# Windowed attention beside a gated MLP: probabilities of units 3 to 15 transposed by VectorE and two transfers through DRAM in place of TensorE

## The chip, the core and the metric

One core of a Trainium2 chip. TensorE (PE in the profile) multiplies matrices into PSUM; VectorE (DVE), ScalarE (ACT) and GpSimd (POOL) work element by element; SyncE (SP) issues all transfers. Each engine runs its own instructions in their written order and waits on semaphores for the others. The metric is the device time of one execution in microseconds, the median of three runs.

## What is computed

```python
scores = scale * np.matmul(q, k.transpose(0, 1, 3, 2))      # 8 batches, 8 heads, 576 positions, 64 wide
mask_plain = (rel >= 0) & (rel < window)                    # heads 0-3: the last 32 positions
mask_dil = (rel >= 0) & (rel < window * dilation) & (rel % dilation == 0)   # heads 4-7: every fourth of 128
scores = np.where(masks[None, :, :, :], scores, -1000000000.0)
attn = np.exp(scores - max); attn = attn / (sum + 1e-09)
out = np.matmul(attn, v)
x = out.transpose(0, 2, 1, 3).reshape(B * S, H * D)         # 4608 tokens of 512
rms = np.sqrt(np.mean(x * x, axis=-1, keepdims=True) + 1e-06)
xn = x / rms * rms_g
g = xn @ w_gate; val = xn @ w_val                           # 512 -> 1536
return silu(g) * val @ w_out                                # 1536 -> 512
```

All of it is float32.

## The kernel before

The 4608 tokens are cut into 16 units of 288 (half a batch). While the MLP of one unit runs, the attention of the next is done in between. Float32 products are made of three float32r products: each operand is split into a high part (ScalarE's cast) and a low part (the rest, `k_lo`, `q_lo` L361-L365, `vhl` L324, `hlo` L749 on GpSimd, `xlo` partly on VectorE), and `three` (L674) multiplies high by high, high by low and low by high.

**The MLP's steps.** A unit has 12 blocks of 128 hidden columns, and each block three steps (L858 on): `gate(u, j)`, `val(u, j)`, and `proj` of the block before. Each step is 12 matmuls of 288 columns. Gate and value of a block take two PSUM banks in turn (`bank`, L692): gate of block j+1 writes the bank that value of block j wrote, so its first matmul waits until the product (`prod`, L735, L737: silu(g) times value, VectorE) of block j has read that. Ahead of the product lie ScalarE's tanh (L719) and VectorE's silu (L724); behind it ScalarE's `hhi` (L748) and GpSimd's `hlo` (L749), which the projection needs two steps later.

**The bursts.** A unit's attention is 14 bursts, each one block of queries of two heads: three blocks of 96 queries for each of two pairs of plain heads, four classes of 72 for each of two pairs of dilated heads. A burst named 5_3_1 is unit 5, pair 3, block 1. Its stages: two score matmuls (L524, float32r, the key's high and low part side by side); one step later VectorE adds the mask to the low product (L381) and takes the maximum with the high one (L386); then ScalarE's exp (L401), VectorE's sum and reciprocal (L410, L411), GpSimd's scaling (L417, `scores_norm`). Six steps behind the scores (`BEHIND`), TensorE transposes the probabilities of both heads (L497) into free columns of a gate bank or a bank of its own; ScalarE evicts the high part (L477) and VectorE the low part (L479, `untranspose`). Ten steps behind the scores, the output matmuls (L512) multiply by v's two parts, and VectorE gathers the result (L439, L441, `take`). Bursts follow every second step, from 11 steps ahead of a unit's first gate to 15 after it.

**What sets the order.** The program is written by hand: `later(dt, rank, fn)` puts a piece of work into the list of a later step, `flush` emits a step's list by rank ahead of the step's matmuls, and each engine keeps that order. `plan` (L808) fixes each burst's steps. Units 0 to 2 (`NEX` = 3) do their attention in plain float32 with other code, which the change leaves on TensorE.

Of the kernel before, what the change touches and what calls it, by code (L numbers as in the profile page):

```python
# [14 lines left out]
ALU = mybir.AluOpType  # L15
# [42 lines left out]
EARLY, LAST = -11, 15  # L58
BEHIND = 6, 10
DONE = 25  # L60
# [17 lines left out]
def attn_moe(ctx: ExitStack, tc: tile.TileContext, qk_in, v_in, w_gate, w_val, w_out, rms_g, outT):  # L78
# [235 lines left out]
    def split_v(b, dt):  # L314
        k = everything.index(b) % 2

        def hi():
            if k not in vparts:
                vparts[k] = late[0].tile([P, 2, 2, D], F32R, name=f"vhl_{k}", bufs=1)
            A.copy(out=vparts[k][:, :, 0], in_=vs[b])  # L320

        def lo():
            vp = vparts[k]
            G.tensor_tensor(out=vp[:, :, 1], in0=vs.pop(b), in1=vp[:, :, 0], op=ALU.subtract)  # L324
            load_v(further(b, 3))

        later(dt, 3.3, hi)
        later(dt, 5.1, lo)
# [6 lines left out]
    def split(u, h, when, ek, eq):  # L335
# [11 lines left out]
        def k_hi():  # L347
            ks = tile(2 * KW, "ks").rearrange("p (t k) -> p t k", t=2)
            A.copy(out=ks[:, 0, :nkt], in_=kr)
            got.append(ks)  # L350

        def k_lo():
            ks = got[0]
            ek.tensor_tensor(out=ks[:, 1, :nkt], in0=kr, in1=ks[:, 0, :nkt], op=ALU.subtract)  # L354

# [5 lines left out]
        def q_lo():  # L361
            ks, qs = got
            eq.tensor_tensor(out=qs[D:], in0=qr[D:], in1=qs[D:], op=ALU.subtract)  # L363
            heads[u, h] = (qs, ks)
            if after(u, h, 2):  # L365
                load(*after(u, h, 2))

# [6 lines left out]
    def scores_max(u, c, i, s_ps):  # L374
        blocks, nq, _ = geometry(u, c)
        _, _, mc, n = blocks[i]
        sv = s_ps[:QB].rearrange("q (a t k) -> q a t k", a=2, t=2)
        other = u < NNAT and everything.index((u, c, i)) % 4 == 3
        t = sb.tile([QB, 2, P], F32, tag="qs" if other else "t", name=f"t_{u}_{c}_{i}", bufs=3)
        if u >= NEX:  # L380
            V.tensor_tensor(out=t[:nq, :, :n], in0=sv[:nq, :, 1, :n],  # L381
                            in1=mask[:nq, None, mc:mc + n].to_broadcast([nq, 2, n]), op=ALU.add)
        sm = sums[everything.index((u, c, i)) % len(sums)]
        for a in range(2):
            plus = t[:nq, a, :n] if u >= NEX else mask[:nq, mc:mc + n]
            V.tensor_tensor_reduce(out=t[:nq, a, :n], in0=sv[:nq, a, 0, :n], in1=plus,  # L386
                                   op0=ALU.add, op1=ALU.min,
                                   scale=-(0.5 if u == NNAT else 1.0) / math.sqrt(D),
                                   scalar=3e38, accum_out=sm[:nq, a, 0:1])
        st[u, c, i] = t, sm  # L390

    def by_rows(u, c, i):
# [3 lines left out]
    def scores_exp(u, c, i):  # L396
        blocks, nq, _ = geometry(u, c)
        n = blocks[i][3]
        t, sm = st[u, c, i]
        for a in range(2):  # L400
            A.activation(out=t[:nq, a, :n], in_=t[:nq, a, :n], func=AF.Exp, scale=-1.0,  # L401
                         bias=sm[:nq, a, 0:1], accum_out=None if by_rows(u, c, i) else sm[:nq, a, 1:2])

    def scores_norm(u, c, i):
# [65 lines left out]

    def untranspose(b, t_ps, wait):
        blocks, nq, _ = geometry(*b[:2])
        n = blocks[b[2]][3]
        t_in = t_ps[:n].rearrange("k (a q) -> k a q", a=2)[:, :, :nq]
        exact = b[0] < NEX
        st[b] = pt = sb.tile([P, 2, 2, QB], F32 if exact else F32R, tag="pt", name=f"pt_{b[0]}_{b[1]}_{b[2]}", bufs=2)
        A.copy(out=pt[:n, 0, :, :nq], in_=t_in)  # L477
        def low_part():
            V.tensor_tensor(out=pt[:n, 1, :, :nq], in0=t_in, in1=pt[:n, 0, :, :nq], op=ALU.subtract)  # L479

        if not exact:
            later(1, 0.4 if wait > 1 else -1.5, low_part) if wait else low_part()

    def products(q, t, o, t_ps, s_tag="s", o_tag="o", wait=0):
# [30 lines left out]
        def scored(a):  # L515
# [7 lines left out]
            qs, ks = heads[q[0], 2 * q[1] + a]  # L523
            PE.matmul(sv[:nq, a, :, :n], qs[:, qc:qc + nq], ks[:, :, kc:kc + n], start=True, stop=True)  # L524
# [8 lines left out]
        if t:  # L533
            later(1, 0.2, lambda: untranspose(t, t_ps, wait))
        if o:
# [322 lines left out]
    for u in range(NU):  # L858
        for j in range(NJ):
            for part in range(0 if u + j else 2, 3):  # L860
# [16 lines left out]
                else:  # L877
# [79 lines left out]
```

## Time and profile before

| | |
|---|---|
| median of three runs | 1105.96 us (1104.24 to 1106.1) |
| profiled execution | 1103.95 us; its span 1102.2 us |
| granted TensorE clock | 1.00 of full speed |
| GpSimd's busy time, hlo (L749) and both splits (L354, L363) | 145.2, 96.8 and 84.3 us of 670.1 |
| VectorE's busy time, silu and products (L724, L737), gathering (L439, L441) | 80.8 and 79.8, 117.1 and 101.1 us of 782.7 |
| DMA | 82.18 MB, mean 75 GB/s |

How to read it: a row in order of time has its start and length in us, engine, line, operation, output and inputs, and in brackets how long the engine stood idle before it and what ended that. A row of a group ends in its busy time in us, the mean length of one in ns, and idle time before. A row of stretches gives each engine's busy time (and instructions) in order PE, PE's weight loads, DVE, ACT, POOL, then the granted clock, the DMA share and GB/s. Matmuls overlap, so one's length says little; the distance from start to start says what it costs.

### The profile page before, as it was taken

Reading aid. Unit: us, or ns where it says so; the run is one execution under the profiler, and the core shown is the slowest. Engines: PE = TensorE matmul, PEld = TensorE weight load, DVE = VectorE, ACT = ScalarE, POOL = GpSimd, SP = SyncE. Lnnn points to the kernel's source line nnn. Section 1 sums busy time; section 2 is a strip of 40 time slices with the busy share of each in tenths; the row PEclk is TensorE's granted clock in tenths of the full one; section 3 lists DMA queues with packets and bytes.
Section 4 is the critical chain, followed back from the end, with each engine's and each line's share of the span. In section 5 each row is a group of like instructions: output and inputs, shape, how many; then the busy total and the mean of one; then the engine's idle time right before and its main releaser. Section 6 shows DMA issues by size and latency. Waiting matters only on the chain.

```text
span 1102.2 us, 25627 instructions
## 1 busy us (share of the span) xinstructions
PE 1095.2 (99%) x8416; PEld 1071.6 (97%) x8416; DVE 782.7 (71%) x3094; ACT 614.8 (56%) x2202; POOL 670.1 (61%) x1152
## 2 busy tenths in 40 slices
PE   8999999999999999999999999999999999999998
PEld 7787999999999999999999999999999999999998
DVE  7988667868687676867768677686867768687412
ACT  6895676556465564646556464664646556464211
POOL 6333589657585675757657575775758657584211
PEclk9999999999999999999999999999999999999999
DMA  9774213212131131312212131131212212120000
GB/s 255 205 263 163 79 51 87 74 35 82 43 94 52 41 97 30 95 42 73 66 36 85 43 94 43 50 96 37 79 43 83 64 32 83 53 74 13 18 6 22
DMA packets 61543, 82.18 MB, mean 75 GB/s; under 512 B 7298, under 2 KB 41090, under 8 KB 61410
## 3 DMA queue, kind: packets, MB, share of 16 engines
q1 hardware_dynamic: 61410, 80.54, 24.3%
q8 instruction: 67, 1.10, 0.4%
q14 instruction: 66, 0.54, 0.2%
HBM read 71.08 MB, written 9.44 MB: 73 GB/s over the span
## 4 chain that ended last, share of the span: by engine, by line
PE 95%; POOL 2%; DVE 1%; ACT 1%; issue 1%; POOLq 0%; ACTq 0%; DVEq 0%
PE acc L682 17%; PE g L682 17%; PE v L682 17%; PE acc L679 9%; PE g L679 9%; PE v L679 9%; PE o L512 3%; PE s L524 3%; PE acc L676 2%; PE v L676 2%; PE g L676 2%; PE t L497 2%; PE s L521 1%; PE g L497 1%; PE busy L802 1%; PE o L509 1%
## 5 line engine op out<-in xcount | busy, mean ns | idle before, releaser
L749 POOL TENSOR_TENSOR hlo<-th,hhi 128x288 fp32r<-128x288 f32 x179 | 145.2, 811 | 161.3 <-ACT hhi L748 147.8
L401 ACT ACTIVATE t<-t,sum 96x128 f32<-96x128 f32 (+3 forms) x448 | 165.9, 374 | 107.8 <-DVE sum L386 105.1
L682 PE MATMUL acc<-hhi,lo 128*128 128x288 f32 x720 | 212.7, 295 | 0.0
L417 POOL TENSOR_SCALAR t<-t,sum 96x128 f32<-96x128 f32 (+3 forms) x416 | 147.6, 366 | 88.4 <-DVE sum L411 74.6
L719 ACT ACTIVATE th<-g 128x288 f32<-128x288 f32 x180 | 73.8, 410 | 195.2 <-PE g L682 100.5
L682 PE MATMUL g<-xhi,lo 128*128 128x288 f32 x612 | 180.3, 295 | 0.0
L682 PE MATMUL v<-xhi,lo 128*128 128x288 f32 x612 | 180.2, 294 | 0.0
L439 DVE TENSOR_REDUCE xraw<-o 64x72 f32<-64x144 f32 (+1 forms) x364 | 117.1, 322 | 84.0 <-PE o L512 79.5
L724 DVE SCALAR_TENSOR_TENSOR th<-th,g 128x288 f32<-128x288 f32 x180 | 80.8, 449 | 102.0 <-ACT th L719 78.4
L682 PEld LDWEIGHTS acc<-hhi,lo 128*128 128x128 f32 x720 | 135.4, 188 | 0.0
L324 POOL TENSOR_TENSOR vhl<-vt,vhl 128x128 fp32r<-128x128 f32 x182 | 84.4, 464 | 70.4 <-ACT vhl L320 66.8
L748 ACT CAST hhi<-th 128x288 fp32r<-128x288 f32 x180 | 77.7, 432 | 75.5 <-DVE th L737 74.6
L682 PEld LDWEIGHTS g<-xhi,lo 128*128 128x128 f32 x612 | 115.2, 188 | 0.0
L682 PEld LDWEIGHTS v<-xhi,lo 128*128 128x128 f32 x612 | 115.1, 188 | 0.0
L737 DVE TENSOR_TENSOR th<-th,v 128x288 f32<-128x288 f32 x180 | 79.8, 444 | 43.6 <-PE v L682 43.5
L441 DVE TENSOR_TENSOR xraw<-o,xraw 64x72 f32<-64x72 f32 (+1 forms) x364 | 101.1, 278 | 12.5
L679 PE MATMUL acc<-hhi,hi_o 128*128 128x288 f32 x360 | 109.0, 303 | 0.0
L679 PE MATMUL g<-xhi,hi_g 128*128 128x288 f32 x357 | 107.0, 300 | 0.0
L682 PE MATMUL acc<-hlo,hi_o 128*128 128x288 f32 x360 | 106.4, 296 | 0.0
L363 POOL TENSOR_TENSOR qs<-qk,qs 64x288 fp32r<-64x288 f32 x104 | 84.3, 811 | 24.1 <-ACT qs L358 16.9
L354 POOL TENSOR_TENSOR ks<-qk,ks 128x288 fp32r<-128x288 f32 (+2 forms) x104 | 96.8, 936 | 3.1
L682 PE MATMUL g<-xlo,hi_g 128*128 128x288 f32 x322 | 95.1, 295 | 0.0
(193 smaller groups left out, 3458.6 us busy)
## 6 DMA issues: line engine op xcount, KB each, us to landing
qk<-in_qk_dram SPq DMA_DIRECT2D x60, 288.0 KB, 2.9
vt<-in_v_dram SPq DMA_DIRECT2D x196, 64.0 KB, 1.9
qk<-in_qk_dram SPq DMA_DIRECT2D x30, 352.0 KB, 2.9
out_dram<-ot SPq DMA_DIRECT2D x64, 144.0 KB, 1.9
qk<-in_qk_dram SPq DMA_DIRECT2D x30, 304.0 KB, 2.9
raw<-in_w_gate_dram SPq DMA_DIRECT2D x12, 512.0 KB, 4.6
raw<-in_w_val_dram SPq DMA_DIRECT2D x12, 512.0 KB, 3.3
raw<-in_w_out_dram SPq DMA_DIRECT2D x12, 512.0 KB, 4.2
```

The lines of the kernel that those rows point to most:

```text
L324: G.tensor_tensor(out=vp[:, :, 1], in0=vs.pop(b), in1=vp[:, :, 0], op=ALU.subtract)
L354: ek.tensor_tensor(out=ks[:, 1, :nkt], in0=kr, in1=ks[:, 0, :nkt], op=ALU.subtract)
L363: eq.tensor_tensor(out=qs[D:], in0=qr[D:], in1=qs[D:], op=ALU.subtract)
L401: A.activation(out=t[:nq, a, :n], in_=t[:nq, a, :n], func=AF.Exp, scale=-1.0, bias=sm[:nq, a, 0:1], accum_out=None if by_rows(u, c, i) els ...
L417: (V if u == 0 and (c, i) > (NC - 1, 1) else G).tensor_scalar(out=t[:nq, a, :n], in0=t[:nq, a, :n], scalar1=sm[:nq, a, 3:4], scalar2=1.0, ...
L439: V.tensor_reduce(out=ours, in_=o[:D, cols:cols + 2 * nq].rearrange("d (t q) -> d q t", t=2), axis=mybir.AxisListType.X, op=ALU.add)
L441: V.tensor_tensor(out=ours, in0=o[D:, cols:cols + nq], in1=ours, op=ALU.add)
L679: PE.matmul(out, wh[:, cc, :], xh, start=start, stop=False)
L682: PE.matmul(out, w[:, cc, :], v, start=False, stop=stop and k == 1)
L724: V.scalar_tensor_tensor(out=t, in0=t, scalar=1.0, in1=g, op0=ALU.add, op1=ALU.mult)
L737: V.tensor_tensor(out=t, in0=t, in1=v_ps[:, :U], op=ALU.mult)
L749: (V if (u, j) == (NU - 1, NJ - 1) else G).tensor_tensor(out=lo, in0=t, in1=hi, op=ALU.subtract)
```

## The change

From unit 3 on, no burst is transposed by TensorE. Once the probabilities are scaled, VectorE transposes the tile of 96 queries by 2 x 128 keys in squares of 32 x 32, in place. A first transfer writes it to DRAM (2 x 96 rows of 512 bytes), and a second, which waits for the first, reads it back with the key on the partition, in pieces of 32 queries (768 pieces of 128 bytes). ScalarE casts the high part and VectorE makes the low part, as before, but from SBUF. The stages stand at steps 5, 5, 6, 9 and 9 behind the scores (`TURN`); the output stays at 10.

So that the second transfer finds keys in order, keys are kept in four classes: the splitting of k reads every fourth column and writes the classes one after another (L346 on), the scores' moving operand has eight runs in place of two, and the mask is rearranged once. Tiles whose burst has fewer than 96 queries or 128 keys are first filled with zeros by GpSimd (`begin`), when the scores are issued. One more tile of probabilities is kept, one less for v (two, not three); the loads of q, k and v are put one step later, behind the transfers.

```diff
-BEHIND = 6, 10
+OUTPUT = 10
+TURN = (5, 4), (5, 9.5), (6, 9.5), (9, 0.2), (9, 0.9)
...
-            vt = sb.tile([P, 2, D], F32, tag="vt", name=f"vt_{u}_{c}_{i}", bufs=3)
+            vt = sb.tile([P, 2, D], F32, tag="vt", name=f"vt_{u}_{c}_{i}", bufs=2)
...
-            A.copy(out=ks[:, 0, :nkt], in_=kr)
+            A.copy(out=ks[:, 0, :nkt].rearrange("p (c k) -> p c k", c=4), in_=kr.rearrange("p (k c) -> p c k", c=4))
...
-            ek.tensor_tensor(out=ks[:, 1, :nkt], in0=kr, in1=ks[:, 0, :nkt], op=ALU.subtract)
+            hi, lo = (ks[:, t, :nkt].rearrange("p (c k) -> p c k", c=4) for t in range(2))
+            ek.tensor_tensor(out=lo, in0=kr.rearrange("p (k c) -> p c k", c=4), in1=hi, op=ALU.subtract)
...
-                load(*after(u, h, 2))
+                later(1, 9.9, lambda: load(*after(u, h, 2)))
...
+            t = blank.pop((u, c, i))
+            tk, mk = keys(t, n), mask.rearrange("q (c k) -> q c k", c=4)[:, :, mc // 4:(mc + n) // 4]
...
+            V.tensor_tensor(out=tk[:nq], in0=low[:nq], in1=mk[:nq].to_broadcast(list(tk[:nq].shape)), op=ALU.add)
...
+    def begin(b):
+        _, nq, _ = geometry(*b[:2])
+        n = geometry(*b[:2])[0][b[2]][3]
+        pool, bufs = (late[0], 1) if late and everything.index(b) % 4 == 3 else (sb, 3)
+        blank[b] = t = pool.tile([QB, 2, P], F32, tag="t", name=f"t_{b[0]}_{b[1]}_{b[2]}", bufs=bufs)
+        if nq < QB or n < P:
+            G.memset(t, 0.0)
...
+    def turn(b):
...
+        def squares():
+            t = st[b][0]
+            V.transpose(out=t, in_=t)
+        def put():
+            t, _ = st.pop(b)
+            d = dr.tile([2, QB, P], F32, tag="turn", name=f"turn_{b[0]}_{b[1]}_{b[2]}")
+            nc.sync.dma_start(out=d.rearrange("a q k -> q a k"), in_=t)
+            got.append(d)
+        def get():
+            st[b] = pt = sb.tile([P, 2, 2, QB], F32R, tag="pt", name=f"pt_{b[0]}_{b[1]}_{b[2]}", bufs=2)
+            squares = got.pop().rearrange("a (r i) (c j) -> (i c) (a r) j", i=W, j=W)
+            nc.sync.dma_start(out=pt[:, 1].bitcast(F32).rearrange("k a (r j) -> k (a r) j", j=W), in_=squares)
+        def high():
+            pt = st[b]
+            A.copy(out=pt[:n, 0, :, :nq], in_=pt[:n, 1, :, :nq].bitcast(F32))
+        def low():
+            pt = st[b]
+            V.tensor_tensor(out=pt[:n, 1, :, :nq], in0=pt[:n, 1, :, :nq].bitcast(F32), in1=pt[:n, 0, :, :nq], op=ALU.subtract)
+        for (dt, rank), fn in zip(TURN, (squares, put, get, high, low)):
+            later(dt, rank, fn)
...
+            kk = ks[:, :, :nkt].rearrange("p t (c k) -> p t c k", c=4)[..., kc // 4:(kc + n) // 4]
...
-        t_at, o_at = ([t + n for t in q_at] for n in BEHIND)
+        t_at, o_at = [None] * nb, [t + OUTPUT for t in q_at]
```

**Where instructions move.** The first place is GpSimd, around the low parts of the next unit's k while the scores of 5_3_1 are made (`hlo_4_3` is the hidden block 3 of unit 4; `ks_6_0` and `ks_6_1` are k of unit 6, `qs` its q, `t` the probabilities). Before:

```order
L749 TENSOR_TENSOR hlo_4_3_5038<-th_4_3_4995,hhi_4_3_5037 128x288
L354 TENSOR_TENSOR ks_6_0_5008<-qk_6_0_4812,ks_6_0_5008 128x288
L354 TENSOR_TENSOR ks_6_1_5010<-qk_6_1_4849,ks_6_1_5010 128x288
L363 TENSOR_TENSOR qs_6_0_5041<-qk_6_0_4812,qs_6_0_5041 64x288
L324 TENSOR_TENSOR vhl_0_2294<-vt_5_2_2_4890,vhl_0_2294 128x2x64
L417 TENSOR_SCALAR t_5_3_0_5004<-t_5_3_0_5004,sum0_86 72x104 x2
L363 TENSOR_TENSOR qs_6_1_5081<-qk_6_1_4849,qs_6_1_5081 64x288
```

And with the change, at the same place:

```order
L812 TENSOR_TENSOR hlo_4_3_5112<-th_4_3_5070,hhi_4_3_5111 128x288
L357 TENSOR_TENSOR ks_6_0_5082<-qk_6_0_4916,ks_6_0_5082 128x288
L357 TENSOR_TENSOR ks_6_1_5084<-qk_6_1_4959,ks_6_1_5084 128x288
L418 MEMSET t_5_3_1_5141 96x256
L366 TENSOR_TENSOR qs_6_0_5115<-qk_6_0_4916,qs_6_0_5115 64x288
L326 TENSOR_TENSOR vhl_0_2300<-vt_5_2_2_5047,vhl_0_2300 128x2x64
L447 TENSOR_SCALAR t_5_3_0_5068<-t_5_3_0_5068,sum0_88 72x4x26 x2
L366 TENSOR_TENSOR qs_6_1_5154<-qk_6_1_4959,qs_6_1_5154 64x288
L418 MEMSET t_5_3_2_5209 96x256
```

A memset of each burst's tile now stands in the queue, behind hlo and whatever part of a split falls into the step.

The second place is VectorE, between the maximum of 5_3_1 and the product of block 4 of unit 4. Before:

```order
L386 ISA t_5_3_1_5074,sum1_87<-s_5_3_1_5058,t_5_3_1_5074 72x104
L386 ISA sum1_87 72x1
L410 TENSOR_REDUCE sum0_86<-sum0_86 72x2
L411 RECIPROCAL sum0_86<-sum0_86 72x2
L724 SCALAR_TENSOR_TENSOR th_4_4_5104<-th_4_4_5104,g_4_4_5087 128x288
L737 TENSOR_TENSOR th_4_4_5104<-th_4_4_5104,v_4_4_5112 128x288
```

With the change:

```order
L400 ISA t_5_3_1_5141,sum1_89<-s_5_3_1_5135,t_5_3_1_5141 72x4x26
L400 ISA sum1_89 72x1
L533 TENSOR_TENSOR pt_5_2_1_5045<-pt_5_2_1_5045 104x2x72
L514 STREAM_TRANSPOSE t_5_2_3_5006<-t_5_2_3_5006 96x256
L439 TENSOR_REDUCE sum0_88<-sum0_88 72x2
L440 RECIPROCAL sum0_88<-sum0_88 72x2
L787 SCALAR_TENSOR_TENSOR th_4_4_5178<-th_4_4_5178,g_4_4_5161 128x288
L800 TENSOR_TENSOR th_4_4_5178<-th_4_4_5178,v_4_4_5190 128x288
```

The low part stands here and not between the gathering instructions, and a transpose in squares is new between the maximum and the product.

The third place is SyncE's queue at the same burst, whose rows were loads alone. Before:

```order
L293 DMA qk_6_0_4812<-in_qk_dram 128x576
L301 DMA vt_5_2_1_4819<-in_v_dram 128x128
L293 DMA qk_6_1_4849<-in_qk_dram 128x576
L301 DMA vt_5_2_2_4890<-in_v_dram 128x128
L301 DMA vt_5_2_3_4953<-in_v_dram 128x128
```

With the change:

```order
L295 DMA qk_6_0_4916<-in_qk_dram 128x576
L303 DMA vt_5_2_0_4918<-in_v_dram 128x128
L519 DMA turn_5_2_0_4957<-t_5_2_0_4783 96x2x128
L295 DMA qk_6_1_4959<-in_qk_dram 128x576
L525 DMA pt_5_2_0_4983<-turn_5_2_0_4957 128x6x32
L303 DMA vt_5_2_1_4985<-in_v_dram 128x128
L519 DMA turn_5_2_1_5025<-t_5_2_1_4864 96x2x128
L525 DMA pt_5_2_1_5045<-turn_5_2_1_5025 128x6x32
```

Each burst has two more transfers there, and the second waits for the first to land and for the output matmuls of the burst two before, with the loads behind it in the queue.

More of the change, by code (lines that the diff above doesn't have):

```diff
@@ L87, in attn_moe @@
     ps = ctx.enter_context(tc.tile_pool(name="ps", bufs=1, space=PSUM))
+    dr = ctx.enter_context(tc.tile_pool(name="dr", bufs=2, space=bass.MemoryType.DRAM))
     ident = cst.tile([QB, QB], F32, name="ident")
@@ L324, in lo @@
             G.tensor_tensor(out=vp[:, :, 1], in0=vs.pop(b), in1=vp[:, :, 0], op=ALU.subtract)
-            load_v(further(b, 3))
+            later(1, 9.9, lambda: load_v(further(b, 2)))
         later(dt, 3.3, hi)
@@ L378, in scores_max @@
         other = u < NNAT and everything.index((u, c, i)) % 4 == 3
[L379 to L382, printed above, removed]
+        if u < NEX:
+            t = sb.tile([QB, 2, P], F32, tag="qs" if other else "t", name=f"t_{u}_{c}_{i}", bufs=3)
+        else:
+            t = blank.pop((u, c, i))
+            tk, mk = keys(t, n), mask.rearrange("q (c k) -> q c k", c=4)[:, :, mc // 4:(mc + n) // 4]
+            low = sv[:, :, 1, :n]
+            if n == P:
+                mk = mk.rearrange("q c i -> q (c i)")[:, None]
+            else:
+                mk, low = mk[:, None], low.rearrange("q a (c i) -> q a c i", c=4)
+            V.tensor_tensor(out=tk[:nq], in0=low[:nq], in1=mk[:nq].to_broadcast(list(tk[:nq].shape)), op=ALU.add)
         sm = sums[everything.index((u, c, i)) % len(sums)]
         for a in range(2):
-            plus = t[:nq, a, :n] if u >= NEX else mask[:nq, mc:mc + n]
-            V.tensor_tensor_reduce(out=t[:nq, a, :n], in0=sv[:nq, a, 0, :n], in1=plus,
+            out, scores, plus = t[:nq, a, :n], sv[:nq, a, 0, :n], mask[:nq, mc:mc + n]
+            if u >= NEX:
+                out = plus = tk[:nq, a]
+                if n < P:
+                    scores = scores.rearrange("q (c i) -> q c i", c=4)
+            V.tensor_tensor_reduce(out=out, in0=scores, in1=plus,
                                    op0=ALU.add, op1=ALU.min,
@@ L390, in scores_max, with keys @@
         st[u, c, i] = t, sm
+    def keys(t, n):
+        return t[:, :, :n] if n == P else t.rearrange("q a (c i) -> q a c i", i=W)[..., :n // 4]
+    blank = {}
+    def begin(b):
[5 more added lines that the diff above has]
+            G.memset(t, 0.0)
     def by_rows(u, c, i):
@@ L469, in attn_moe, with untranspose @@
     everything = [b for u in range(NU) for b in bursts(u)]
-    def untranspose(b, t_ps, wait):
+    def untranspose(b, t_ps):
         blocks, nq, _ = geometry(*b[:2])
         n = blocks[b[2]][3]
[L474 to L482, printed above, removed]
+        st[b] = pt = sb.tile([P, 2, 2, QB], F32, tag="pt", name=f"pt_{b[0]}_{b[1]}_{b[2]}", bufs=2)
+        A.copy(out=pt[:n, 0, :, :nq], in_=t_ps[:n].rearrange("k (a q) -> k a q", a=2)[:, :, :nq])
+    def turn(b):
+        blocks, nq, _ = geometry(*b[:2])
+        n = blocks[b[2]][3]
+        got = []
+        def squares():
[15 more added lines that the diff above has]
+            pt = st[b]
+            V.tensor_tensor(out=pt[:n, 1, :, :nq], in0=pt[:n, 1, :, :nq].bitcast(F32), in1=pt[:n, 0, :, :nq],
+                            op=ALU.subtract)
+        for (dt, rank), fn in zip(TURN, (squares, put, get, high, low)):
+            later(dt, rank, fn)
     def products(q, t, o, t_ps, s_tag="s", o_tag="o", wait=0):
@@ L533, in products @@
         if t:
-            later(1, 0.2, lambda: untranspose(t, t_ps, wait))
+            later(1, 0.2, lambda: untranspose(t, t_ps))
         if o:
@@ L541, in products @@
             if o[0] < NEX:
-                later(1, 9, lambda: load_v(further(o, 3)))
+                later(1, 9, lambda: load_v(further(o, 2)))
             far = further(o, 2)
@@ L551, in products @@
             u, c, i = q
+            if u >= NEX:
+                begin(q)
+                turn(q)
+                if q == (NEX, 0, 0):
+                    t = sb.tile([QB, 2, P], F32, tag="t", name="by_four", bufs=3)[:, 0]
+                    A.copy(out=t.rearrange("q (c k) -> q c k", c=4), in_=mask.rearrange("q (k c) -> q c k", c=4))
+                    A.copy(out=mask, in_=t)
             nxt = after(u, 2 * c, 2)
@@ L810, in plan @@
             for kind, t in zip("qto", ts):
-                events.setdefault(base + t, {})[kind] = b
+                if t is not None:
+                    events.setdefault(base + t, {})[kind] = b
         last = base + (o_at[-1] if u < NNAT else DONE)
@@ L881, in attn_moe @@
                     free = None
-                if part == 2 or part == 1 and events.get(now[0], {}).get("t", (0,))[0] >= NEX:
-                    if "t" in events.get(now[0], {}):
-                        free = ps.tile([P, 512], F32, tag=bank("g", j), name=f"t_{u}_{j}")[:, :2 * QB]
+                if part == 2 and "t" in events.get(now[0], {}):
+                    free = ps.tile([P, 512], F32, tag=bank("g", j), name=f"t_{u}_{j}")[:, :2 * QB]
                 attend(free, s_tag="acc2" if t < 4 else "s", wait=(1, 2, 0)[part])
```

12 lines of the change are left out of this document (7 added, 5 removed).

## The prediction

> **What bounds the kernel now.** I read the page first, then TensorE in order of time, then VectorE and GpSimd in the stretch where attention and the MLP run side by side. The page's first lines and its chain of waits:
>
> ```profile
> span 1102.2 us, 25627 instructions
> PE 1095.2 (99%) x8416; PEld 1071.6 (97%) x8416; DVE 782.7 (71%) x3094; ACT 614.8 (56%) x2202; POOL 670.1 (61%) x1152
> ...
> PE 95%; POOL 2%; DVE 1%; ACT 1%; issue 1%; POOLq 0%; ACTq 0%; DVEq 0%
> ```
>
> TensorE is busy 99% of the span and carries 95% of the chain, so an instruction taken from it shortens the kernel by its own slot, if nothing else becomes late. Whether something does is not read from 71%. From the first output matmuls of a unit to its last scores VectorE has far more to do. The next view is busy time in five stretches of such a passage (columns: TensorE, weight loads, VectorE, ScalarE, GpSimd). Each stretch runs from the end of one product of L737 to the end of the next. The second answer's sum is the same passage one unit earlier, where the keys are the shorter kind:
>
> ```profile
> 320.59:327.54 6.95, 6.95 (x57) 6.95 (x56) 6.43 (x28) 5.60 (x21) 6.06 (x11) 1.00 0.61 184
> 327.54:331.86 4.32, 4.32 (x38) 4.32 (x37) 3.45 (x16) 2.37 (x10) 3.19 (x7) 1.00 0.35 98
> 331.86:338.72 6.86, 6.86 (x57) 6.86 (x55) 5.60 (x26) 3.81 (x16) 2.62 (x6) 1.00 0.09 29
> 338.72:342.98 4.26, 4.26 (x38) 4.26 (x37) 3.36 (x16) 2.87 (x11) 3.98 (x7) 1.00 0.04 12
> 342.98:349.79 6.81, 6.81 (x56) 6.81 (x55) 5.56 (x27) 3.46 (x15) 4.88 (x11) 1.00 0.43 119
> sum 29.20, PE 29.20 PEld 29.20 DVE 24.41 ACT 18.10 POOL 20.73; mean PE 5.84 PEld 5.84 DVE 4.88 ACT 3.62 POOL 4.15
> ```
> ```profile
> sum 28.85, PE 28.85 PEld 28.85 DVE 23.31 ACT 17.36 POOL 19.62; mean PE 5.77 PEld 5.77 DVE 4.66 ACT 3.47 POOL 3.92
> ```
>
> VectorE is 84% busy here, and its instructions start 0.03 to 0.04 us after one another. What it truly waits is only this (one row for each wait; the first stretch has the 0.2, the short ones the two of 0.3 each, the long ones the 0.9):
>
> ```profile
> DVE xraw L439 <- PE o L512: 0.2, 1, 0.2
> DVE th L737 <- PE v L682: 0.3, 1, 0.3
> DVE xraw L439 <- PE o L512: 0.3, 1, 0.3
> DVE xraw L439 <- PE o L512: 0.9, 1, 0.9
> ```
>
> So VectorE's work, gaps between instructions included, is 6.75, 3.7, 5.95, 3.65 and 5.9 us. TensorE needs its product in time: a gate group writes the bank that the product before it reads. The first matmuls of the gate groups:
>
> ```profile
> 322.11 0.30 PE L679 MATMUL g<-xhi,hi_g 128*128 128x288 f32 x1
> ...
> 328.01 0.31 PE L679 MATMUL g<-xhi,hi_o 128*128 128x288 f32 x1
> ...
> 333.34 0.29 PE L679 MATMUL g<-xhi,hi_g 128*128 128x288 f32 x1
> ...
> 339.14 0.31 PE L679 MATMUL g<-xhi,hi_g 128*128 128x288 f32 x1
> ...
> 344.45 0.30 PE L679 MATMUL g<-xhi,hi_v 128*128 128x288 f32 x1
> ...
> 350.01 0.38 PE L679 MATMUL g<-xhi,hi_o 128*128 128x288 f32 x1
> ```
>
> The products end 1.52, 0.47, 1.48, 0.42, 1.47 and 0.22 us ahead of them. Every second margin is under half a microsecond. That is what the change must not use up.
>
> **What it takes away.** One burst (two heads of a block) is two output matmuls, two transposes, two score matmuls. Starts of transposes and scores in a burst of 96 queries and in one of 72, and a row that counts the bursts of the units concerned:
>
> ```profile
> 327.65 0.33 PE L497 MATMUL t<-ident,t 96*128 96x96 f32 x2
> 327.76 0.41 PE L524 MATMUL s<-ks,qs 128*72 128x208 f32 x2
> ...
> 412.01 0.29 PE L497 MATMUL g<-ident,t 72*72 72x72 f32 x2
> 412.10 0.33 PE L524 MATMUL s<-ks,qs 128*72 128x144 f32 x2
> ```
> ```profile
> L324 POOL TENSOR_TENSOR vhl<-vt,vhl 128x128 fp32r<-128x128 f32 x182 | 84.4, 464 | 70.4 <-ACT vhl L320 66.8
> ```
>
> The pair takes 0.11 and 0.09 us of TensorE's time, since matmuls overlap: 0.10. 182 bursts x 0.10 = 18.2 us. The evictions stay: ScalarE's and VectorE's parts of the probabilities now read SBUF, for the same columns.
>
> **What it adds to VectorE.** One transpose in squares for each burst, 96 x 256 elements. No row shows one. The nearest is an addition of the same size; with it, from VectorE in order of time, the reductions and additions that gather an output and the mask addition of burst 3_1:
>
> ```profile
> L381 DVE TENSOR_TENSOR t<-s,mask 96x256 f32<-96x256 f32 x66 | 27.5, 417 | 1.2
> ```
> ```profile
> 327.85 0.35 DVE L439 TENSOR_REDUCE xraw<-o 64x96 f32<-64x192 f32 x1 [0.31 <-PE o L512]
> 328.23 0.26 DVE L441 TENSOR_TENSOR xraw<-o,xraw 64x96 f32<-64x96 f32 x1
> ...
> 339.02 0.30 DVE L439 TENSOR_REDUCE xraw<-o 64x72 f32<-64x144 f32 x1 [0.30 <-PE o L512]
> 339.36 0.29 DVE L441 TENSOR_TENSOR xraw<-o,xraw 64x72 f32<-64x72 f32 x1
> ...
> 340.73 0.37 DVE L381 TENSOR_TENSOR t<-s,mask 72x208 f32<-72x208 f32 x1
> ```
>
> I take 0.42 and the gap, 0.45 us. At the low end 0.30, as the 144-element reduction (one input from SBUF and no arithmetic could be quicker); at the high end 0.85, if a square is written only after it is read. In VectorE's order it stands behind the masked maximum and ahead of the next product, so it lies on the way to the gate group.
>
> **What it adds to GpSimd.** 116 memsets of 96 x 256: in all 13 units for the eight bursts of the dilated heads, and in six for the first blocks of the plain ones. VectorE's mask addition into the same tile waits for it. Memset rows, and GpSimd in order of time before bursts 2_2 and 3_1 of the unit quoted:
>
> ```profile
> L263 POOL MEMSET qk<- 64x576 f32 x5 | 2.6, 572 | 0.1
> ...
> L101 POOL MEMSET mask<- 96x128 f32 x1 | 0.2, 201 | 0.0
> ```
> ```profile
> 328.10 0.81 POOL L749 TENSOR_TENSOR hlo<-th,hhi 128x288 fp32r<-128x288 f32 x1
> 328.99 0.81 POOL L363 TENSOR_TENSOR qs<-qk,qs 64x288 fp32r<-64x288 f32 x1
> ...
> 339.27 0.81 POOL L749 TENSOR_TENSOR hlo<-th,hhi 128x288 fp32r<-128x288 f32 x1
> 340.04 1.58 POOL L354 TENSOR_TENSOR ks<-qk,ks 128x288 fp32r<-128x288 f32 x2
> ```
>
> Between 128 and 576 columns the price grows by 0.83 ns a column, so 0.31 us each. The memset of 2_2 is queued behind hlo and qs: it ends at 328.99 + 0.81 + 0.31 = 330.1. VectorE, once late, does two reductions and two additions after the product that ends at 327.54, 2 x (0.35 + 0.26) and gaps, 1.36 us, and asks for it at 328.9: a wait of 1.2. The memset of 3_1 stands behind hlo and both low parts of k: 340.04 + 1.58 + 0.31 = 341.9. VectorE asks at 338.72 + 2 x (0.30 + 0.29) and gaps = 340.0, a wait of 1.9. Even in this trace the addition started at 340.73, ahead of that end. Behind the waiting addition stand the maximum, the low part, the transpose, silu and the next product. The chain cannot be hurried: hlo needs hhi, which needs the product itself.
>
> The low parts of k now read every fourth element. No row steps like this; bounds are nothing and another 0.8 us each, and I take nothing, as unit-stride and halved reads on GpSimd differ little here. In the Trainium skill, "GPSIMD Engine Reference", section "Performance pitfalls for Q7 kernels", a read step of over 8 bytes costs some 2.9 cycles an element in place of 1.9; at its 1.2 GHz that is an estimate of 0.24 us for each of the two parts ahead of 3_1, 0.48 a unit and 6 us in all, which would make the forecast below 1142. No run here shows it yet.
>
> **The sum.** Gate spacings lose 0.10 for each burst inside: 5.70, 5.23, 5.60, 5.21, 5.36. VectorE gains 0.90 where two transposes fall in a stretch, 0.45 where one does. The product ahead of the first margin had waited 0.19:
>
> ```profile
> 320.13 0.46 DVE L737 TENSOR_TENSOR th<-th,v 128x288 f32<-128x288 f32 x1 [0.19 <-PE v L682]
> ```
>
> So that margin, 1.52, shrinks by one transpose less 0.19, and by 0.10: 1.16.
> First gate: 6.75 + 0.90 - 1.16 - 5.70 = 0.79 late, and TensorE stalls for it.
> Second: 3.7 + 0.45 + 1.2 - 5.23 = 0.14.
> Third: 5.95 + 0.90 - 5.60 = 1.25.
> Fourth: 3.65 + 0.45 + 1.9 - 5.21 = 0.79.
> Fifth: 5.9 + 0.90 - 5.36 = 1.44.
> Together 4.4 us. After it no scores are left and VectorE recovers. A unit of the other kind: VectorE idles 28.85 - 23.31 = 5.54 in place of 29.20 - 24.41 = 4.79, so 0.75 less: 3.7. Six units of each carry both waits; the last has no next keys to split and keeps 1.3. 6 x 4.4 + 6 x 3.7 + 1.3 = 50 us. The profiled execution took 1103.95 us (span 1102.2 and 1.75 around it), 2 under the median 1105.96. 1103.95 - 18.2 + 50 = 1136.
>
> **Costed at nothing.** The scores' moving operand comes in eight runs in place of two: 57 matmuls fill 6.95 us, 0.12 each, most of them of 288 columns, the score matmuls of 144 to 256, so a slower read has cover; without it half as much again on 364 of them, 22 us. ScalarE's strided copy of k: ScalarE is busy 56%. Two loads in place of three for v: covered while SP is prompt. The transfers: rows for nearby ones.
>
> ```profile
> q1 hardware_dynamic: 61410, 80.54, 24.3%
> ...
> vt<-in_v_dram SPq DMA_DIRECT2D x196, 64.0 KB, 1.9
> ```
>
> The first transfer lands in about 1.9 us. The second is 768 packets of 128 B: from 1.9 (as the v load) to 5.3 us (1.9, and 48 packets for each of 16 engines at this trace's mean, 0.243 x 1102.2 x 16 / 61410 = 0.07 us). It leaves when the output two bursts before has freed its tile, and ScalarE asks for it behind the tanh two steps later, some two thirds of a gate spacing and a little: 4.1 by estimate. I take 3, and the cover holds.
>
> **Rivals.**
> *VectorE is late by its own transposes alone.* GpSimd's memsets come in time: then margins of about 1.1 survive each short stretch, and a unit loses 1.3 or 0.6. 1103.95 - 18.2 + 13 = 1099. For it: GpSimd idles 39% of the span. Against: both queues above are already longer than VectorE's.
> *The whole gain.* Transposes of 0.3 us or less that fall into waits: 1086. Against: VectorE waits under 0.9 us in every stretch.
> *The trip through DRAM is too slow.* At 5.3 us the second transfer is 1.2 late; ScalarE, then VectorE's low part wait in five stretches of 13 units, 75 us on top: about 1210. It decides from 4.1 us. For it stands, in the Trainium skill, "DMA: Bandwidth & Descriptors", section "Specifications": transfers under 512 B are below line rate, since they read, modify and write. Against: the 512-byte rows of the v loads land in 1.9.
>
> **How the numbers follow.** Late memsets and transposes together (1136): 0.62. VectorE alone (1099): 0.20. The whole gain: 0.06. DRAM: 0.08. The rest, 0.04, is about no change. Within the first case a transpose of 0.30 takes 14 us off (eight a unit, 12 units) and one of 0.85 adds 38; the k parts add 6 or more, and margins I missed take some off. The range 1094 to 1165 holds that case and most of the second. About 0.2% is what a measurement of this kernel can tell from no change. Faster 0.24, the same 0.05, slower 0.71.
>
> **What would show it.** Right: gate groups stall on VectorE's product, five times a unit, some 4 us together; VectorE waits for GpSimd's memset before the mask addition, 1 to 2 us, twice a unit; transposes of about 0.42. Wrong: TensorE still without a gap; transposes under 0.3 us or over 0.8; waits of ScalarE for a transfer; score matmuls further apart than now.

## The result and the profile after

| | before | after |
|---|---|---|
| median | 1105.10 us (4 runs, 1103.91 to 1106.10) | 1157.96 us (4 runs, 1157.26 to 1159.31) |
| ratio, with its 95% interval | | 1.048 (1.0462 to 1.0498) |
| span of the profiled execution | 1102.2 us | 1155.5 us |

The change makes the kernel 53 us slower. The forecast was 1136, with a range of 1094 to 1165. The page of the kernel after, its first lines and its chain:

```profile
span 1155.5 us, 26558 instructions
PE 1101.5 (95%) x8052; PEld 1051.2 (91%) x8052; DVE 850.6 (74%) x3276; ACT 662.6 (57%) x2204; POOL 722.5 (63%) x1268
...
PE 54%; DVE 21%; POOL 12%; issue 7%; ACT 5%; DMA 2%; POOLq 0%; DVEq 0%; ACTq 0%; SPq 0%
```

TensorE has 364 matmuls less and idles 54 us where it idled 7. Its share of the chain falls from 95% to 54%, and VectorE and GpSimd carry a third of it. The list of waits of the kernel after (us in total, times, longest), the rows that lead to TensorE:

```profile
ACT pt L529 <- DMA pt<-turn: 82.9, 86, 3.0
...
DVE t L392 <- POOL t L418: 50.7, 25, 2.5
...
PE o L567 <- DVE pt L533: 33.4, 36, 1.5
...
PEld o L567 <- POOL qs L366: 22.1, 19, 1.7
...
PEld g L742 <- DVE th L800: 14.7, 43, 0.5
...
PEld o L567 <- POOL vhl L326: 12.7, 10, 1.5
```

VectorE waits for 25 of the 116 memsets (not each of the 182 bursts has one), twice in nearly every unit, 2.0 us each. TensorE waits mostly at the output matmuls (L567), 33.4 us for the low part of the probabilities, and less at the gate groups. The rows of PEld are the weight loads ahead of the same matmuls: they show the same stalls over again and are not to be added. One of these waits in order of time, on VectorE, GpSimd, TensorE and its weight loads:

```profile
339.42 0.26 DVE L471 TENSOR_TENSOR xraw<-o,xraw 64x96 f32<-64x96 f32 x1
341.81 0.37 DVE L392 TENSOR_TENSOR t<-s,mask 72x208 f32<-72x208 f32 x1 [2.13 <-POOL t L418]
...
342.60 0.35 DVE L533 TENSOR_TENSOR pt<-pt 128x192 fp32r<-128x192 f32 x1
```
```profile
339.72 0.80 POOL L812 TENSOR_TENSOR hlo<-th,hhi 128x288 fp32r<-128x288 f32 x1
340.60 0.81 POOL L366 TENSOR_TENSOR qs<-qk,qs 64x288 fp32r<-64x288 f32 x1
341.47 0.31 POOL L418 MEMSET t<- 96x256 f32 x1
```
```profile
341.69 0.29 PE L745 MATMUL v<-xhi,lo 128*128 128x288 f32 x1
343.20 0.44 PE L567 MATMUL o<-pt,vhl 128*128 128x192 f32 x2 [1.22 <-DVE pt L533]
```
```profile
341.86 0.46 POOL L326 TENSOR_TENSOR vhl<-vt,vhl 128x128 fp32r<-128x128 f32 x1
...
343.17 0.30 PEld L567 LDWEIGHTS o<-pt,vhl 128*128 128x128 f32 x2 [1.42 <-POOL vhl L326]
```

The memset stands behind hlo and q's low part and ends at 341.78. VectorE had nothing else from 339.68 on. Behind its mask addition stand the maximum and the low part, which ends at 342.95. TensorE, ready at 341.83, starts the output matmul at 343.20. The weight load's row names GpSimd's vhl, but that ended at 342.32; what came last is the low part.

From the first eviction of one unit's output to that of the next, a unit takes 65.9 us before, and 69.6 to 70.7 after.

### The profile page after: what moved, and what is told of

Its sections match the earlier page's. It is cut to its first block, busy times and chain, and to the rows that moved or that the text cites. A ratio compares the mean times of both kernels' runs of the same rounds, so it can differ in the third digit from the quotient of the medians.

```text
span 1155.5 us, 26558 instructions
## 1 busy us (share of the span) xinstructions
PE 1101.5 (95%) x8052; PEld 1051.2 (91%) x8052; DVE 850.6 (74%) x3276; ACT 662.6 (57%) x2204; POOL 722.5 (63%) x1268
## 4 chain that ended last, share of the span: by engine, by line
PE 54%; DVE 21%; POOL 12%; issue 7%; ACT 5%; DMA 2%; POOLq 0%; DVEq 0%; ACTq 0%; SPq 0%
PE g L745 10%; PE acc L745 9%; PE v L745 8%; PE g L742 5%; PE acc L742 5%; PE v L742 4%; POOL ks L357 4%; DVE t L392 3%; DVE xraw L469 3%; PE o L567 3%; DVE pt L533 2%; POOL qs L366 2%; DVE t L514 2%; DVE th L800 2%; DVE t L400 2%
## 5 line engine op out<-in xcount | busy, mean ns | idle before, releaser
L326 POOL TENSOR_TENSOR vhl<-vt,vhl 128x128 fp32r<-128x128 f32 x182 | 87.6, 481 | 77.5 <-ACT vhl L322 65.3
L357 POOL TENSOR_TENSOR ks<-qk,ks 128x288 fp32r<-128x288 f32 (+2 forms) x104 | 111.5, 1077 | 3.1
L567 PE MATMUL o<-pt,vhl 128*128 128x192 f32 (+3 forms) x364 | 71.3, 278 | 39.5 <-DVE pt L533 33.4
L567 PEld LDWEIGHTS o<-pt,vhl 128*128 128x128 f32 (+3 forms) x364 | 56.4, 188 | 56.6 <-POOL qs L366 22.1
L392 DVE TENSOR_TENSOR t<-s,mask 96x256 f32<-96x256 f32 (+3 forms) x182 | 66.9, 367 | 55.1 <-POOL t L418 50.7
L529 ACT CAST pt<-pt 128x192 fp32r<-128x192 f32 (+3 forms) x182 | 59.2, 325 | 83.7 <-DMA pt<-turn 82.9
```

Of the source, the lines that this page charges most:

```text
L357: ek.tensor_tensor(out=lo, in0=kr.rearrange("p (k c) -> p c k", c=4), in1=hi, op=ALU.subtract)
L392: V.tensor_tensor(out=tk[:nq], in0=low[:nq], in1=mk[:nq].to_broadcast(list(tk[:nq].shape)), op=ALU.add)
L567: PE.matmul(o_ps[:, 2 * a * nq:2 * (a + 1) * nq].rearrange("d (t q) -> d t q", t=2), vp[:n, a].rearrange("k t d -> k (t d)"), pt[:n, :, a, ...
```

## The experiments

Nine kernels in which one or two parts were undone or one was done alone, and three that look for a better one. In the diffs, `...` stands for lines that are not shown. Medians are of 4 runs (8 in the last); the kernel before had 1104.16 to 1104.45 beside them. All theories agree on TensorE's saving; the **main theory** is that of the forecast, late memsets and VectorE's transposes.

**Zeros written once.** Four tiles are kept for the probabilities and filled only at their first use.

```diff
...
-        if nq < QB or n < P:
+        if b[0] == NEX and everything.index(b) < 14 * NEX + 4:
             G.memset(t, 0.0)
...
```

> The kernel after, with GpSimd filling the four probability tiles with zeros once, at their first use in unit 3, and never again. Late memsets (main theory): VectorE's 25 waits for a memset, 50.7 us, go, and with them most of the output matmuls' waits for the low part; 1100 to 1115 us. DRAM trip as the cause: ScalarE still waits some 83 us for the second transfer and the output matmuls still wait; 1140 us or more. VectorE's own transposes as the only cost left: the forecast's second case, about 1099.

Measured: 1123.45 us, ratio 1.0172 (1.0157 to 1.0188). The memsets cost 34.5 us. Two of its waits:

```profile
ACT pt L529 <- DMA pt<-turn: 110.8, 119, 3.4
...
PE o L567 <- DVE pt L533: 7.3, 16, 0.7
```

ScalarE waits for the landing more than ever, 111 us, and yet TensorE's wait for the low part is down from 33.4 to 7.3. The main theory holds for two thirds of the loss. But 1123 is above its 1115, so it isn't all.

**No trip through DRAM.** Put and get are left out; high and low part come from two tiles of zeros that stay.

```diff
-            nc.sync.dma_start(out=d.rearrange("a q k -> q a k"), in_=t)
...
-            nc.sync.dma_start(out=pt[:, 1].bitcast(F32).rearrange("k a (r j) -> k (a r) j", j=W), in_=squares)
+            st[b] = flat[k]
```

> The kernel after without both transfers of the probabilities: the high and low parts are taken from two tiles of zeros that stay, so the attention's output is zero. Late memsets: VectorE still waits some 50 us for them, and the output matmuls with it; 1140 to 1158 us. DRAM trip as the cause: ScalarE's 83 us of waits for the landing go; 1085 to 1125 us.

Measured: 1156.53 us, ratio 1.0473 (1.0457 to 1.0489): 1.4 us less than with the trip. The waits that matter stand as they did:

```profile
DVE t L392 <- POOL t L418: 51.7, 26, 2.4
...
PE o L567 <- DVE pt_flat L533: 35.7, 50, 1.3
```

The trip is not the cause: 1.4 us are little more than the runs of one kernel scatter (1155.6 to 1157.3 here). ScalarE's 83 us of waits were time that it had.

**VectorE's transposes alone, in the kernel before.** TensorE's transposes stay. Three tiles are kept for the probabilities and filled with zeros once.

```diff
...
+            if q[0] >= NEX:
+                later(5, 4, lambda: V.transpose(out=st[q][0], in_=st[q][0]))
```

> The kernel before, with VectorE's transpose in squares added in place at step 5 behind the scores, TensorE's transposes kept, no memset in a loop, no transfer (the probabilities come out in the wrong order). Late memsets: by the margins of before, the first gate of a unit is 0.5 us late and the others meet theirs, 12 units x 0.5 = 6 us: 1107 to 1114. VectorE's transposes as the main cost: 1125 or more. VectorE has room for them: 1105.

Measured: 1117.85 us, ratio 1.0125 (1.0108 to 1.0142). The row:

```profile
L557 DVE STREAM_TRANSPOSE t<-t 96x256 f32<-96x256 f32 x182 | 79.4, 436 | 0.8
```

13.6 us for 182 transposes of 0.436 us. That is more than the 6 that this run was given from the gates' margins; part of it is TensorE's wait at its own transposes for silu and product (at 347.67 us the first starts 0.48 us behind the output matmul, where 0.11 is usual), a place that the margins did not include. From the last output matmul of a burst to its first transpose TensorE spends 5.6 us more in sum than in the kernel before, nearly half of the 12.2 by which the profiled span is longer. The kernel after has no such transposes, so this part of the 13.6 can't be taken over to it as it stands.

**The four classes alone, in the kernel before.** k's parts read every fourth column, scores with eight runs.

```diff
-            A.copy(out=ks[:, 0, :nkt], in_=kr)
+            A.copy(out=ks[:, 0, :nkt].rearrange("p (c k) -> p c k", c=4), in_=kr.rearrange("p (k c) -> p c k", c=4))
...
```

> The kernel before, with k's high and low parts read at every fourth column and the scores' moving operand in eight runs (mask left as it was, so the result is another one). All theories that cost this at nothing: 1105, within 2. Eight runs slow the score matmuls: 22 us, 1127. GpSimd's strided read holds up its queue: 0.14 us for each of 104 low parts is 15 us of GpSimd, of which nearly none shows while TensorE is busy 99%: 1105 to 1111.

Measured: 1115.51 us, ratio 1.0102 (1.0087 to 1.0117). 11.2 us where nothing or nearly nothing was expected. The casts of ScalarE in the kernel before and here (ns, shortest, median, longest):

```profile
L349 ACT CAST ks<-qk x104: 415/446/543, 156.6 to 982.3; 128x288 fp32r<-128x288 f32 x48, 128x320 fp32r<-128x320 f32 x28, 128x416 fp32r<-128x416 f32 x28
```
```profile
L349 ACT CAST ks<-qk x104: 700/756/961, 156.7 to 992.2; 128x288 fp32r<-128x288 f32 x48, 128x320 fp32r<-128x320 f32 x28, 128x416 fp32r<-128x416 f32 x28
```

Reading and writing in strides makes the cast 0.3 us longer, two thirds more; GpSimd's low parts go from a median of 872 to 1032 ns. The score matmuls don't suffer: the stretch from the last matmul ahead of a burst of two outputs, two transposes and two scores to the first behind it has a median of 0.65 us, 0.64 before. Where it shows, once in every second unit (VectorE, GpSimd and TensorE of this run):

```profile
451.87 1.33 DVE L664 TENSOR_TENSOR xlo<-xraw,xhi 128x288 fp32r<-128x288 f32 x1 [0.18 <-ACT xhi L663]
```
```profile
451.57 1.31 POOL L355 TENSOR_TENSOR ks<-qk,ks 128x416 fp32r<-128x416 f32 x1
```
```profile
454.20 0.40 PE L683 MATMUL v<-xhi,hi_g 128*128 128x288 f32 x1 [0.39 <-DVE pt L480]
456.49 0.38 PE L498 MATMUL t<-ident,t 96*128 96x96 f32 x2 [0.24 <-DVE th L728]
```

VectorE's subtraction of x, with a median of 0.46 us, takes 1.33: it has both inputs in SBUF, and ends 0.32 us after GpSimd's low part of k. The same place in the kernel before, on VectorE and on GpSimd:

```profile
447.89 0.46 DVE L660 TENSOR_TENSOR xlo<-xraw,xhi 128x288 fp32r<-128x288 f32 x1 [0.18 <-ACT xhi L659]
```
```profile
444.50 1.08 POOL L354 TENSOR_TENSOR ks<-qk,ks 128x416 fp32r<-128x416 f32 x1
...
447.92 1.37 POOL L354 TENSOR_TENSOR ks<-qk,ks 128x416 fp32r<-128x416 f32 x1
```

There VectorE starts 0.03 us ahead, and it is GpSimd's instruction that takes 0.29 longer than its twin of the other head. Some tenths of a microsecond in ScalarE's and GpSimd's queues have turned the order round. From the first eviction of one unit's output to that of the next it takes 1.4 us longer than before in every second unit, six times, 8.4 of the 9.8 us by which this span is longer. That the turned order is how the strided work comes to cost this is read from the trace, not separated by a run.

**The low part from SBUF alone, in the kernel before.** This one followed from the last: after the change VectorE's low part has both inputs in SBUF too, where one was in PSUM. Here the high part is taken from itself, so that the low part is zero.

```diff
-            V.tensor_tensor(out=pt[:n, 1, :, :nq], in0=t_in, in1=pt[:n, 0, :, :nq], op=ALU.subtract)
+            V.tensor_tensor(out=pt[:n, 1, :, :nq], in0=pt[:n, 0, :, :nq].bitcast(F32), in1=pt[:n, 0, :, :nq], op=ALU.subtract)
```

> The kernel before, with one operand changed: VectorE's low part reads both inputs from SBUF (the high part twice, so that it is zero) and none from PSUM. If a VectorE instruction with two inputs in SBUF has to wait while GpSimd reads SBUF: some of the 182 low parts take 0.5 to 1.1 us in place of 0.35, and the time is 1108 to 1117 us (12 us are what the sum 1104 - 18 + 13.5 + 11.2 + 34.5 leaves open against the 1158 measured). If both sources cost the same: 1103 to 1106.

Measured: 1112.96 us, ratio 1.0078 (1.0063 to 1.0093), 8.5 us for one operand. The low part in the kernel before (two rows, by the bank that was read), and here:

```profile
L479 DVE TENSOR_TENSOR pt<-t,pt x117: 281/308/360, 179.7 to 1014.2; 128x192 fp32r<-128x192 f32 x40, 104x144 fp32r<-104x144 f32 x35, 72x144 fp32r<-72x144 f32 x30, 96x192 fp32r<-96x192 f32 x12
L479 DVE TENSOR_TENSOR pt<-g,pt x65: 296/300/350, 183.1 to 1017.9; 128x192 fp32r<-128x192 f32 x26, 104x144 fp32r<-104x144 f32 x21, 72x144 fp32r<-72x144 f32 x18
```
```profile
L479 DVE TENSOR_TENSOR pt<-pt x182: 282/410/1101, 179.9 to 1027.2; 128x192 fp32r<-128x192 f32 x66, 104x144 fp32r<-104x144 f32 x56, 72x144 fp32r<-72x144 f32 x48, 96x192 fp32r<-96x192 f32 x12
```

With an input in PSUM the longest of 182 takes 0.36 us; with both in SBUF the longest takes 1.10, the shortest no longer than before. One long one, and GpSimd beside it:

```profile
318.39 1.10 DVE L479 TENSOR_TENSOR pt<-pt 128x192 fp32r<-128x192 f32 x1
```
```profile
317.58 0.92 POOL L417 TENSOR_SCALAR t<-t,sum 96x128 f32<-96x128 f32 x2
318.47 0.80 POOL L749 TENSOR_TENSOR hlo<-th,hhi 128x288 fp32r<-128x288 f32 x1
319.35 0.81 POOL L363 TENSOR_TENSOR qs<-qk,qs 64x288 fp32r<-64x288 f32 x1
```

It ends at 319.49, 0.22 after hlo, as if most of it had waited until hlo was through. Of the 168 low parts from 240 us on, 60 take over a quarter more than the median, 16.2 us too much together, and each of the 60 runs beside a subtraction of GpSimd; in the kernel before none takes that long. In the Trainium skill, "SBUF — State Buffer", section "Who interferes with whom", a VectorE instruction with two SBUF inputs contends with a GpSimd instruction that reads SBUF, since its second input comes through the shared interface, and the order of issue decides who waits. The traces agree on the contention, with all of these 60 and none in the kernel before. On the order, the two rows of before agree, where the low part of k that started second was the one drawn out; the row at 318.39 doesn't show it, since hlo starts 0.08 us behind it and still ends first.

Most of what it costs stands at one place, in every second unit:

```profile
PE t L497 <- DVE th L724: 5.0, 6, 0.9
```

These are TensorE's own transposes, which wait for silu. From output matmuls to transposes TensorE spends 6.7 us more in sum than before, of the 9.2 by which this span is longer. The kernel after has no such place.

**The low part ahead of the mask addition**, in the kernel after: rank 0.65 in place of 0.9 in `TURN`.

```diff
-TURN = (5, 4), (5, 9.5), (6, 9.5), (9, 0.2), (9, 0.9)
+TURN = (5, 4), (5, 9.5), (6, 9.5), (9, 0.2), (9, 0.65)
```

> The kernel after, with VectorE's low part one place earlier: ahead of the mask addition that waits for the memset, not behind it and the maximum. If the stall is made by that place in the queue: the output matmuls' wait for the low part (33 us) falls under 10, the memset waits stay, part of them comes back at the gates; 1135 to 1148 us. If VectorE is late by its sum whatever the order: the stall only moves to the gate groups; 1152 to 1160.

Measured: 1159.4 us, ratio 1.0499 (1.0482 to 1.0517). Its waits:

```profile
PEld s L581 <- PE o L567: 31.2, 70, 1.1
...
DVE t L392 <- POOL t L418: 28.4, 21, 2.2
...
PEld g L742 <- DVE th L800: 24.6, 46, 0.8
PE s L581 <- DVE sum L400: 23.8, 53, 1.1
...
PE g L742 <- DVE th L800: 14.7, 34, 0.7
```

The outputs hardly wait any more, and nothing is won: the score matmuls now wait 23.8 us for the maximum (0.2 in the kernel after) and the gate groups 14.7 for the product (4.0). TensorE idles 54 us of the span in both kernels. VectorE is late by its sum; the place in its queue only chooses who waits.

**k laid in four classes in DRAM beforehand**, in the kernel after, so that cast and low part run in line.

```diff
...
-                    qk_in[u, h, rows, U:U + nkt] = k[b, h, ki].T
+                    qk_in[u, h, rows, U:U + nkt] = k[b, h, ki if u < NEX else ki.reshape(-1, 4).T.ravel()].T
```

> The kernel after, with k's columns of units 3 to 15 laid in four classes in DRAM beforehand, so that ScalarE's cast and GpSimd's low part read and write in line (the scores' operand still has eight runs). If the strided casts and low parts cost what they cost in the kernel before (11 us): 1145 to 1150. If they hide behind the waits for the memset: 1154 to 1158.

Measured: 1143.08 us, ratio 1.0352 (1.0337 to 1.0368), 14.9 less than the kernel after, more than the 11.2 alone. GpSimd's low parts of k stand ahead of the memset, but VectorE's waits for the memset fall only from 50.7 to 47.0 us, so by which path the 14.9 come is not shown.

**Zeros once and no trip; zeros once and k laid beforehand.**

> Zeros written once, and no transfers of the probabilities (high and low part from two tiles of zeros, output zero). If the trip through DRAM is covered with the memsets gone too: 1119 to 1124, as with zeros once. If ScalarE's 111 us of waits for the landing there have become the bound: 1112 or less.

> Zeros written once, and k's columns laid in four classes beforehand. If the strided work costs the same here as in the kernel before: 1123.5 less 11, 1109 to 1115. If it costs nothing: 1121 to 1124. If with both gone only VectorE's transposes and TensorE's saving are left (+13.6 less 18): 1098 to 1103.

Measured: 1120.56 (1.0146, 1.0131 to 1.0161) and 1120.22 us (1.0145, 1.013 to 1.0161), against 1123.45 with zeros once. The trip is worth 2.9 us even with the memsets gone, so it stays covered. The strided work is worth only 3.2 there, against 14.9 with the memsets: the two costs overlap. In the second of the two the low part shows its collisions more than in the kernel after:

```profile
L533 DVE TENSOR_TENSOR pt<-pt x182: 297/350/1024, 185.4 to 1036.8; 128x192 fp32r<-128x192 f32 x66, 104x144 fp32r<-104x144 f32 x56, 72x144 fp32r<-72x144 f32 x48, 96x192 fp32r<-96x192 f32 x12
```

Of the 168 from 240 us on, 49 take over a quarter more than the median, 15.6 us too much together; in the kernel after 14 do, with 4.6 us.

**The low part on GpSimd**, for all bursts, for every second one, and for five chosen of a unit, each on top of zeros once and k laid beforehand. The diff has the line taken away and the three that stand in its place, one for each kernel.

```diff
-            V.tensor_tensor(out=pt[:n, 1, :, :nq], in0=pt[:n, 1, :, :nq].bitcast(F32), in1=pt[:n, 0, :, :nq],
+            G.tensor_tensor(out=pt[:n, 1, :, :nq], in0=pt[:n, 1, :, :nq].bitcast(F32), in1=pt[:n, 0, :, :nq],
...
+            (G if everything.index(b) % 2 else V).tensor_tensor(out=pt[:n, 1, :, :nq], in0=pt[:n, 1, :, :nq].bitcast(F32), in1=pt[:n, 0, :, :nq],
...
+            (G if everything.index(b) % 14 in (2, 3, 5, 9, 10) else V).tensor_tensor(out=pt[:n, 1, :, :nq], in0=pt[:n, 1, :, :nq].bitcast(F32), in1=pt[:n, 0, :, :nq],
```

> Zeros written once, k laid in four classes beforehand, and the low part of the probabilities on GpSimd in place of VectorE. If VectorE's time (transposes, and its wait for GpSimd in the low parts) is what is left of the loss: VectorE has 0.43 more and 0.35 less for each burst, and the time is 1088 to 1104 us, the first version that beats the kernel before. If GpSimd, with some 0.55 us more for each burst, becomes late itself: 1115 or more.

> As with the low part on GpSimd, but for every second burst alone. VectorE as the bound: between 1120 and the run with all of them on GpSimd, 1100 to 1112 us. GpSimd as the bound: faster than with all of them there.

> As with the low part by turns, but GpSimd makes it for five bursts of a unit (0_2, 1_0, 1_2, 2_3 and 3_0), at whose outputs the traces with all and with half of them on GpSimd showed no wait, and VectorE for the other nine. If what is left is which queue is late at which burst: the waits of bursts 0_1, 2_1 and 3_1 (0.36 to 0.70, 0.1 to 0.3 and 0.3 to 0.7 us a unit with turns) go, 1.0 to 1.4 us a unit: 1093 to 1101 us, faster than the kernel before. If VectorE only grows late again where it takes them back, as with the low part on VectorE alone: 1108 to 1118.

Measured: 1114.28 (1.0082, 1.0065 to 1.0099), 1110.44 (1.0052, 1.0037 to 1.0067) and 1108.91 us (1.0038, 1.0022 to 1.0053). None beats the kernel before. With all on GpSimd, the waits are of another owner:

```profile
PEld o L567 <- POOL pt L533: 29.8, 43, 1.5
PE o L567 <- POOL pt L533: 17.9, 28, 1.3
```

So GpSimd is late in VectorE's place, by its 0.50 us an instruction; half and half is better. My choice of five, read from where each of the two runs had waited, gave 1.5 us of the 9 to 17 expected: waits moved when the assignment did.

## Why the forecast was right in direction and 22 us short

**TensorE's saving: right.** In the kernel before, a burst of outputs and scores alone takes 0.54 us and one with transposes between them 0.64: the forecast's 0.10. No run takes the transposes away and adds nothing.

**VectorE's transposes: right in size.** 0.433 us against 0.42. Alone they cost 13.6 us; the forecast's second case had put them at 13. That these two agree is partly luck: the 13 were at the gates, and nearly half of the 13.6 stands at TensorE's own transposes.

**Late memsets: right, and nearly so in what they cost.** 311 ns against 0.31, twice a unit behind hlo and splits as said. The waits are longer than priced, 2.0 us and not 1.2 and 1.9, 50.7 us against 6 x 2 x 3.1 = 37, but not all of that reaches the end: written once, the zeros give back 34.5 us. The forecast's first case and its second are 50 - 13 = 37 apart. So the two terms that it priced come out at 34.5 + 13.6 = 48 against its 50, and the 22 us lie in what it put at nothing or took as unchanged.

**"Behind the waiting addition stand the maximum, the low part, the transpose, silu and the next product":** right as a list, but the sum followed the lateness only to the last of them. The first that TensorE needs is the low part, and most of the stall stands at the output matmuls (33.4 us) and not at the gates (4.0). "Gate groups stall on VectorE's product, five times a unit" is refuted as a place. As the run with the low part ahead shows, the amount hardly depends on the place.

**"ScalarE's strided copy of k: ScalarE is busy 56%", "I take nothing" for GpSimd's low parts: wrong, the step that failed first.** A share of busy time is no cover for an instruction ahead of a chain. The cast costs 0.28 us more for 288 columns, the low part 0.12 by the means (965 for 843 ns) and 0.14 by the medians (952 for 808). Alone the classes cost 11.2 us; taken out of the kernel after, 14.9. How much of this is the cast's and how much the low part's, no run separates. The Trainium skill's rule on read steps in "GPSIMD Engine Reference", section "Performance pitfalls for Q7 kernels", had pointed the right way; the estimate of 0.24 us from it is 1.7 to 2 times what was measured.

**"The evictions stay: ... now read SBUF, for the same columns": wrong.** The columns are the same and the time is not: 8.5 us alone. What it costs in the kernel after is not shown, where 14 low parts are drawn out and not 60, and the place that cost most of the 8.5 is gone. No low part in the trace of before had both inputs in SBUF, but a neighbour there showed the effect: the low part of k, drawn out from 1.08 to 1.37 us beside VectorE's subtraction of two SBUF tiles.

**The trip at nothing: right**, though ScalarE's waits for the landing, which I had named as a sign against it, did come: 82.9 us. They were the wrong sign; without the transfers 1.4 us are won. **The scores' eight runs at nothing: right**, 0.65 against 0.64 us a burst.

**The sum by measured terms.** 1104.4 - 18.2 + 13.6 (transposes) + 34.5 (memsets) + 11.2 (classes) + 8.5 (low part) + 1.4 (trip) = 1155.4, against 1157.96. That it closes so well is luck in good part: terms taken in different company differ (strided work 11.2, 14.9 or 3.2), since waits overlap, and the 13.6 and 8.5 hold waits at TensorE's transposes that the kernel after doesn't have. Shown by taking parts out of the kernel after are 37.7 of its 52.9 us, for memsets and strided work together. Open remains what is left with zeros once and k laid beforehand: 1120, where transposes, low part and trip make 1104.4 - 18.2 + 13.6 + 8.5 + 2.9 = 1111. Two rivals for it stand untested. ScalarE waits 31.7 us there for v's loads, which have two tiles in place of three. And VectorE's subtraction of x is drawn out once in each of twelve units, to 1.0 us or more, where in the kernel before none into the same tile takes over 0.52. Each time it starts 0.1 us behind GpSimd's low part of k, and so it does in the kernel after, of which this is one place:

```profile
325.57 1.50 DVE L723 TENSOR_TENSOR xlo<-xraw,xhi 128x288 fp32r<-128x288 f32 x1
```
```profile
325.46 1.29 POOL L357 TENSOR_TENSOR ks<-qk,ks 128x416 fp32r<-128x416 f32 x1
```

Above the 0.46 us that it takes in the kernel before, these are 10.5 us of VectorE's time in the kernel after, and still 8.3 with zeros once and k laid beforehand. How much of it TensorE feels, no run shows.

## What to carry to other kernels

When work moves off a saturated engine, follow each new instruction to the first thing that the saturated engine needs behind it, on every queue, and price a change of access pattern or of an operand's memory as an instruction of its own. A wait that is long in the list need not cost anything (83 us of ScalarE's for a landing cost 1.4), and one that costs can't be cured by order alone where the engine is late by its sum. Ask for each two-input instruction of VectorE whether both inputs are now in SBUF, and what GpSimd reads meanwhile.

## What the runs showed of the hardware

- ScalarE's cast, reading every fourth column and writing four quarters of a row: 711 ns in place of 429 for 128 x 288, 944 for 532 at 416. GpSimd's subtraction with the same read: 965 for 843, 1310 for 1154.
- VectorE's transpose of 96 x 256 float32 in squares, in place: 433 ns, about that of an addition of the size (417).
- VectorE with two SBUF inputs beside a subtraction of GpSimd: 0.35 us becomes up to 1.13 in the low part of the probabilities, 0.46 up to 1.5 in that of x.
- Two transfers of 96 KB, the second in 768 pieces of 128 bytes, land in 1.9 and 2.2 us:

```profile
turn<-t SPq DMA_DIRECT2D x182, 96.0 KB, 1.9
pt<-turn SPq DMA_DIRECT2D x182, 96.0 KB, 2.2
```
